# Sixteen transposes of q moved from TensorE to transposing DMAs, in a linear-attention and MLP kernel

## The chip, the cores and the metric

One core of one Trainium2 chip. The metric is the device time of one execution in microseconds (us), the median of several. PE is TensorE, PEld its weight loads, DVE is VectorE, ACT ScalarE, POOL GpSimd (which issues the loads), SP SyncE (which issues stores and transposing DMAs). All times compared below are of runs in the fast state (mean granted clock 0.99 to 1.0).

## The reference

Linear attention without a mask, a norm per head, then a layer norm and an MLP with a residual.

```python
# q, k, v: (8 batches, 8 heads, 576, 64); d_model = 512, hidden = 2048; all float32
kv  = einsum('bhsd,bhse->bhde', k, v)
o   = einsum('bhsd,bhde->bhse', q, kv)
o   = o / sqrt(mean(o*o, -1) + 1e-6) * g_norm
x   = o.transpose(0, 2, 1, 3).reshape(8, 576, 512)
xn  = (x - mean(x)) / sqrt(var(x) + 1e-6) * moe_g_ln
out = x + relu(xn @ w_ch1) @ w_ch2
```

## The kernel before

A batch has 576 rows: four slots of 128 and a fifth of 64, and the fifths of two batches share one tile. So there are 36 tiles of 128 rows: tiles 0 to 3 are batch 0, 4 to 7 batch 1, tile 8 both slots 4, tile 9 begins batch 2. Each tile needs q turned (`qT`, with the head dimension on the partitions). A slot is four blocks of 128x128. Batches 0 and 1 have q turned on PE, through PSUM; from batch 2 on, one DMA turns all five slots, 20 blocks.

```python
def add_q_turn_pe(b, t, deps, key, eng, h0=0, h1=H):
    # PE: four transposes of 128x128 into PSUM; then one copy to qT by VectorE or ScalarE
    ...
def q_turn_dma(b):                                  # batches 2 to 7
    att[b]["qT"] = work.tile([128, 20, 128], bf16, tag="qT", name="qT", bufs=3)
    nc.sync.dma_start_transpose(att[b]["qT"], qp[b % 2].rearrange("p t h d -> p (t h d)"))
...
# batch 2: q lands in qb, two copies on ScalarE reorder it into qp, then the DMA turns it
qperm.append(add("ACT", 0.85, 1.0, ok - 14, load["q", b][0:1] + [adone[b - 2]["qfree"]],
                 lambda t0=t0, t1=t1: q_permute(nc.scalar, b, t0, t1)))
...
turn = add_dma("SP", ok - 12, qperm + load["q", b] + (...), lambda: q_turn_dma(b),
               2.6e3, 1.0, occ=2.98, lat=0.25, tail=0.42)
turn.lag = 5.0 if by_slot else 0.0                  # by_slot is b >= 3: batch 2 has no lag
```

The order of instructions on every engine is fixed beforehand: a small planner in the kernel (`run_plan`) gives every step a cost and emits the steps by their planned start. Its DMAs pass through one first-in-first-out server, a transpose costing it 0.52 us per slot. The chip doesn't know the plan: each engine takes its instructions in that order and waits on semaphores.

Of the kernel before, what the change touches and what calls it, by code (L numbers as in the profile page):

```python
# [14 lines left out]
def kernel(  # L15
# [13 lines left out]
    bf16 = mybir.dt.bfloat16  # L29
# [33 lines left out]
    def no_fifth(b):  # L63
        return fifth(b + 1)
# [19 lines left out]
    work = ctx.enter_context(tc.tile_pool(name="work", bufs=2))  # L84
# [10 lines left out]
    def add(eng, occ, dur, key, deps, fn, dma=None, alloc=None, main=False, lag=0.0):  # L95
        s = Step()
        s.eng, s.occ, s.dur, s.key, s.fn = eng, occ, dur, key, fn
        s.deps = [d for d in deps if d is not None]
        s.dma, s.alloc, s.main, s.frees, s.behind = dma, alloc, main, None, None
        s.start = s.done = None  # L100
        s.lag = lag
        steps.append(s)
        return s
# [82 lines left out]
    def add_dma(eng, key, deps, fn, nbytes, rate, occ=None, lat=None, tail=None):  # L186
        if eng == "POOL":
            s = add(eng, occ or 0.67, 0, key, deps, fn, dma=(1.0, nbytes / rate / 1e3, 0.6))
        else:
            s = add(eng, occ or 0.55, 0, key, deps, fn,  # L190
                    dma=(0.6 if lat is None else lat, nbytes / rate / 1e3,
                         0.75 if tail is None else tail))
        return s
# [26 lines left out]
    qp = [consts.tile([128, 5, H, D], bf16, name=f"qp{i}") for i in range(2)]  # L220
# [56 lines left out]
    pos, okey = {}, {}  # L277
# [14 lines left out]
    att = [dict() for _ in range(B)]  # L292
    done = [dict() for _ in range(N_TILES)]
    adone = [dict() for _ in range(B)]
# [4 lines left out]
    load = {}  # L299
# [6 lines left out]
    def spread(f):  # L306
        ps = psum.tile([128, 512], f32, tag="mm", name="scale_ps", bufs=BANKS["mm"])
        nc.tensor.matmul(ps[:, 0:f.stop - f.start], lhsT=ones, rhs=scales[:, f], start=True, stop=True)
        att[0]["scale", f.start] = ps

    for eng, f, dst in (("ACT", slice(0, Dm), "gl"), ("DVE", slice(Dm, Dm + D), "gn")):
        s = add("PE", *((1.8, 2.0) if dst == "gl" else (0.4, 0.6)), -98, row + [ones_done], lambda f=f: spread(f), alloc="mm")
# [14 lines left out]
    def pool_do(occ, fn, deps=()):  # L327
        return add("POOL", occ, occ + 0.1, 0, deps, fn)
# [13 lines left out]
    def load_w_kv1():  # L342
# [26 lines left out]
    z1 = [pool_do(0.5, f) for f in (  # L369
        lambda: nc.gpsimd.memset(qp[0][no_fifth(0), 4, :, :], 0.0),  # L370
        lambda: nc.gpsimd.memset(qp[1][no_fifth(1), 4, :, :], 0.0),
        lambda: nc.gpsimd.memset(v5[0][no_fifth(0), :, :], 0.0),
        lambda: nc.gpsimd.memset(v5[1][no_fifth(1), :, :], 0.0),
        lambda: nc.gpsimd.memset(kv_pack[1], 0.0),
        lambda: nc.gpsimd.memset(kv_pack[2], 0.0),
    )]
# [32 lines left out]
    def add_q_turn_pe(b, t, deps, key, eng, h0=0, h1=H):  # L409
        w = (h1 - h0) / H  # L410
        s = add("PE", 0.24 * w, 0.24 * w + 0.26, key, [ident] + list(deps), lag=2.0 if t == 4 else 0.0, fn=
                lambda: q_turn_pe(b, t, h0, h1), alloc=("mm", "kvt")[b])
        occ, dur = act_cost(512 * w) if eng == "ACT" else dve_cost(512 * w, 1.92)
        e = add(eng, occ, dur, key, [s],
                lambda: q_turn_out(b, t, h0, h1, nc.scalar if eng == "ACT" else nc.vector))
        s.frees = e
        adone[b].setdefault(("qT", t), []).append(e)

    def q_turn_dma(b):
        att[b]["qT"] = work.tile([128, 20, 128], bf16, tag="qT", name="qT", bufs=3)  # L420
        nc.sync.dma_start_transpose(
            att[b]["qT"], qp[b % 2].rearrange("p t h d -> p (t h d)"))

    def kv_mm(b, hps):
        ps = psum.tile([128, HP, 128], f32, tag="kvt", name="kv_ps", bufs=BANKS["kvt"])
# [218 lines left out]
    for i, (h0, h1) in enumerate(((0, 4), (4, 8))):  # L644
        hps = range(h0 // 2, h1 // 2)
        s = add("PE", 0.7, 0.95, -60 + i, load["v", 0, h0] + [k0p[i]],
                lambda hps=hps, i=i: kv_mm(0, hps), alloc="kvt")
# [9 lines left out]
    load_w_kv1()  # L657
    pool_load(("q", 0, 4), load_fifth(qp[0][:, 4, :, :], q, 0), 180.0, [])
    pool_load(("q", 1, 4), load_fifth(qp[1][:, 4, :, :], q, 1), 180.0, [])
    add_q_turn_pe(0, 4, load["q", 0, 4] + [z1[0]], pos[8] - 50, "DVE")  # L660
    adone[0]["qfree"] = adone[0]["qT", 4][0]


# [1 line left out]
    def plan_batch(b):  # L665
        p = pos[FIRST[b]]
        ok = okey[FIRST[b]]
        kperm = []
        if b == 1:
            for h0, h1 in ((0, 4), (4, 8)):  # L670
                kperm.append(add("ACT", 1.2, 1.35, p - 18, load["k", 1],
                                 lambda h0=h0, h1=h1: k_permute(nc.scalar, 1, h0, h1)))
            for t in range(5):
                key = (p - 17 + 3 * t) if t < 4 else pos[8] - 40
                if t < 4:
                    qperm = add("ACT", *act_cost(512), key, load["q", 1],
                                lambda t=t: q_permute(nc.scalar, 1, t, t + 1))
                    qread = qperm
                else:
                    qperm = load["q", 1, 4][0]  # L680
                add_q_turn_pe(1, t, [qperm, z1[1]], key + 1, ("DVE", "ACT")[t % 2])
            vdeps = load["v", 1]
            adone[1]["qread"] = qread
            adone[1]["qfree"] = adone[1]["qT", 4][0]
        else:
            f = FIRST[b]
            def gate(n):

                if b >= 3:
                    m, i = divmod(n, 4)  # L690
                    pool_do(0.1, lambda: nc.gpsimd.tensor_copy(  # L691
                        mark, blk[m]["xT"][:, 0, i * 128:i * 128 + 1]), done[n]["xT"])
            def gate_turn():
                if b >= 3:
                    pool_do(0.1, lambda: nc.gpsimd.tensor_copy(
                        mark, att[b - 1]["qT"][:, 0, 0:1]), [adone[b - 1]["qfree"]])
            dk = [adone[b - 2]["kvmm"]]
            if b < 4:

                pool_do(0.5, lambda: nc.gpsimd.memset(kp[b % 2][no_fifth(b), 4, :, :], 0.0), dk)  # L700
            gate(f - 7 if b > 3 else 5)
            gate_turn()
            by_slot = b >= 3
            if by_slot:
                pool_load(("k", b), load_slots(kp[b % 2], k, b), rate1, dk)
            else:
                pool_load(("k", b), load_kv(kb, k, b), rate4, dk)
            pool_load(("k", b), load_fifth(kp[b % 2][:, 4, :, :], k, b), 180.0, dk)
            def some_q():
                gate(f - 6 if b > 3 else 6)  # L710
                if by_slot:
                    pool_load(("q", b), load_slots(qp[b % 2], q, b), rate1, [adone[b - 2]["qfree"]])
                else:
                    pool_load(("q", b), load_q(b, 0, 4), rate4, [adone[b - 1]["qread"]])
                pool_load(("q", b), load_fifth(qp[b % 2][:, 4, :, :], q, b), 180.0,
                          [adone[b - 2]["qfree"]])
            def some_v():
                gate(f - 5 if b > 3 else 7)
                pool_load(("v", b), load_kv(vb, v, b), rate4, dk)
                pool_load(("v", b), load_fifth(v5[b % 2], v, b), 100.0, dk)  # L720
            for load_some in (some_v, some_q) if b == 2 else (some_q, some_v):
                load_some()
            for h0, h1 in ((0, 4), (4, 8))[by_slot * 2:]:
                kperm.append(add("ACT", 0.85, 1.0, ok - 16, load["k", b][0:1] + dk,
                                 lambda h0=h0, h1=h1: k_permute(nc.scalar, b, h0, h1)))
            qperm = []
            for t0, t1 in ((0, 2), (2, 4))[by_slot * 2:]:
                qperm.append(add("ACT", 0.85, 1.0, ok - 14, load["q", b][0:1] + [
                    adone[b - 2]["qfree"]], lambda t0=t0, t1=t1: q_permute(nc.scalar, b, t0, t1)))
            for x in kperm + qperm:  # L730
                x.lag = 4.0 if b == 2 else 6.0
            kperm += load["k", b]
            turn = add_dma("SP", ok - 12, qperm + load["q", b] + (
                adone[b - 3].get("outs", []) if b >= 3 else []),
                           lambda: q_turn_dma(b), 2.6e3, 1.0, occ=2.98, lat=0.25, tail=0.42)
            for t in range(5):
                adone[b]["qT", t] = [turn]
            adone[b]["qfree"] = turn
            turn.lag = 5.0 if by_slot else 0.0
            adone[b]["qread"] = qperm[-1] if qperm else None  # L740
            vdeps = load["v", b]
        outs_before = adone[b - 3].get("outs", []) if b >= 3 else []
        s = add("PE", 1.12 if b > 1 else 1.34, 1.35 if b > 1 else 1.57, (p - 17.5 if b == 1 else ok - 4), vdeps + kperm,
                lambda: kv_mm(b, range(HP)), alloc="kvt")
# [214 lines left out]
```

## Time and profile before

The time was 296.15 us (three runs).

| engine | busy us | share of 295.1 us |
|---|---|---|
| PE | 283.1 | 96% |
| DVE | 165.8 | 56% |
| ACT | 143.1 | 49% |

The list of waits for PE: who waited for what, us in total, times, the longest.

```profile
PE kv_ps L429 <- DMA vb<-in_v_dram: 4.3, 1, 4.3
PE scale_ps L308 <- DMA scales<-in_moe_g_ln_dram: 2.3, 1, 2.3
PE mm_ps L598 <- DMA xT<-xc: 0.7, 1, 0.7
PE mm_ps L583 <- ACT xT L540: 0.7, 1, 0.7
PE mm_ps L583 <- DMA w<-in_moe_w_ch_dram: 0.4, 1, 0.4
```

All but the third line lie before 26 us; the third is at 175.9 us. So PE bounds the program from 26 us on. The chain of work that ended last, in order of time (start us, us, what), runs wholly on PE in the stage that the change touches:

```profile
44.42 0.22 PE qT_ps L401 x4
44.65 1.73 PE mm_ps L617 x8
...
47.46 0.22 PE qT_ps L401 x4
47.69 0.86 PE mm_ps L617 x4
48.55 0.22 PE qT_ps L401 x4
48.77 2.59 PE mm_ps L617 x12
...
52.45 0.22 PE qT_ps L401 x4
```

The four `qT_ps` lines are the 16 transposes at issue: 0.22 us for four, 0.89 us in all. A matmul of 512 columns takes 0.216 us of the chain (1.73 / 8), a transpose of 128 columns about 0.056 (0.89 / 16).

The table by stretches for the same stage has start:end, length, busy us of PE, PEld, DVE, ACT and POOL, granted clock, share of the DMA engines' time that packets took (over 1 where packets overlap), and GB/s:

```profile
45.00:50.00 5.00, 5.00 (x34) 2.64 (x33) 4.56 (x12) 1.68 (x4) 0.00 (x0) 1.00 1.59 192
...
55.00:60.00 5.00, 5.00 (x93) 5.00 (x91) 2.66 (x12) 4.67 (x11) 0.43 (x1) 1.00 0.40 116
```

The DMA engines are full of loads until about 55 us (1.59), then nearly idle (0.40). Batch 2's q is the last large load of that queue. Its line in the list of DMA issues between 40 and 43.3 us (kilobytes as written, us from issue to landing):

```profile
qb<-in_q_dram POOLq DMA_DIRECT2D x1, 512.0 KB, 11.7
```

It is issued at 42.6 us and lands at 54.3. The copies on ScalarE that need it begin at 59.5 us and wait for nothing: some 5 us of slack. Batch 2's own turn, 20 blocks (640 KB), is issued at 61.5 us, with no load beside it, and lands after 4.9 us; for some 3 us of these it moves about 215 GB/s.

### The profile page before, as it was taken

The numbers are of one execution on the slowest core, as the hardware profiler recorded it, in microseconds if no ns is written. First come the engines' busy times: TensorE is split into PE (matmuls) and PEld (weight loads), VectorE is DVE, ScalarE is ACT, GpSimd is POOL, SyncE is SP. The second block draws the span as 40 slices with busy tenths as digits, with TensorE's granted clock in tenths as the row PEclk, the third lists the DMA queues.
The fourth block names the chain that finished last, engine by engine and source line by source line (L and its number), as shares of the span: only waits on it lengthen the run. The fifth ranks groups of instructions, "written<-read, shape, count | busy, mean of one in ns | idle before, by whom it ended". The sixth has DMA issues, their size and how long they took to land.

```text
span 295.1 us, 5184 instructions
## 1 busy us (share of the span) xinstructions
PE 283.1 (96%) x2061; PEld 161.1 (55%) x2061; DVE 165.8 (56%) x360; ACT 143.1 (49%) x288; POOL 66.0 (22%) x92
## 2 busy tenths in 40 slices
PE   3799999999999999999999999999999999999995
PEld 1789955877745445444544445544454444444444
DVE  1397038759876886557655773577557755420022
ACT  3178972986857612671267117621762177006500
POOL 8882230208207024320403207020000000000000
PEclk9999999999999999999999999999999999999999
DMA  6999999749999998998399799999201310210012
GB/s 91 176 196 206 203 199 192 181 89 106 188 176 82 139 120 200 161 120 168 93 131 86 107 185 130 137 134 178 56 18 53 91 53 18 56 71 35 0 73 72
DMA packets 107388, 35.21 MB, mean 119 GB/s; under 512 B 85603, under 2 KB 103395, under 8 KB 107364
## 3 DMA queue, kind: packets, MB, share of 16 engines
q0 software_dynamic: 72608, 18.35, 65.2%
q1 hardware_dynamic: 34516, 16.39, 23.5%
q8 instruction: 16, 0.26, 0.4%
q10 hardware_dynamic: 240, 0.13, 0.2%
q14 instruction: 8, 0.07, 0.1%
HBM read 36.70 MB, written 9.44 MB: 156 GB/s over the span
## 4 chain that ended last, share of the span: by engine, by line
PE 87%; DMA 10%; POOL 1%; issue 1%; DVE 1%; ACT 0%; ACTq 0%; POOLq 0%
PE mm_ps L617 39%; PE mm_ps L598 33%; PE mm_ps L583 8%; DMA w<-in_moe_w_ch_dram 4%; DMA xT<-xc 3%; PE kv_ps L429 3%; PE out_ps L452 3%; DMA kb<-in_k_dram 3%; PE xT_ps L533 1%; PE qT_ps L401 0%; POOL qp L254 0%; POOL kb L233 0%; POOL w L334 0%; DVE ss L474 0%; POOL vb L233 0%
## 5 line engine op out<-in xcount | busy, mean ns | idle before, releaser
L617 PE MATMUL mm_ps<-w,m 128*128 128x512 bf16 (+2 forms) x608 | 130.3, 368 | 0.0
L598 PE MATMUL mm_ps<-xT,w 128*128 128x512 bf16 x448 | 100.8, 379 | 0.7 <-DMA xT<-xc 0.7
L605 ACT ACTIVATE m<-mm_ps 128x512 bf16<-128x512 f32 x112 | 66.8, 597 | 51.2 <-PE mm_ps L598 50.2
L617 PEld LDWEIGHTS <-m 128*128 128x128 bf16 x608 | 57.0, 98 | 59.7
L598 PEld LDWEIGHTS <-w 128*128 128x128 bf16 x448 | 43.0, 98 | 49.5 <-issue 1.2
L624 DVE SCALAR_TENSOR_TENSOR x<-mm_ps,rstd,x 128x512 f32<-128x512 f32 (+2 forms) x38 | 27.3, 721 | 41.9 <-PE mm_ps L617 41.8
L474 DVE TENSOR_REDUCE ss<-sq 128x8 f32<-128x512 f32 (+1 forms) x37 | 24.8, 670 | 46.0 <-ACT sq L465 45.9
L465 ACT ACTIVATE sq<-out_ps 128x512 f32<-128x512 f32 (+1 forms) x37 | 21.5, 584 | 52.3 <-PE out_ps L452 52.3
L583 PE MATMUL mm_ps<-xT,w 128*128 128x128 bf16 x512 | 30.9, 219 | 1.0 <-ACT xT L540 0.7
L583 PEld LDWEIGHTS <-w 128*128 128x128 bf16 x512 | 29.3, 98 | 2.1 <-issue 0.8
L526 DVE SCALAR_TENSOR_TENSOR xc<-x,mv,gl 128x512 bf16<-128x512 f32 (+1 forms) x37 | 27.1, 737 | 1.4 <-DVE mv L521 0.3
L469 DVE TENSOR_TENSOR xg<-out_ps,gn 128x512 f32<-128x512 f32 (+1 forms) x37 | 24.8, 669 | 0.3
L691 POOL COPY mark<-xT 128x1 bf16<-128x1 bf16 x15 | 5.1, 340 | 80.4 <-DMA xT<-xc 67.8
L590 ACT ACTIVATE m<-mm_ps 128x512 bf16<-128x512 f32 x32 | 18.3, 597 | 3.2 <-PE mm_ps L583 2.5
L504 DVE TENSOR_TENSOR x<-xg,inv 128x512 f32<-128x512 f32 x24 | 16.6, 693 | 0.8
L520 DVE BATCH_NORM_STATS2 stats<-x 128x6 f32<-128x512 f32 x24 | 16.6, 690 | 0.5
L444 DVE CAST kv_pack<-kv_ps 64x256 bf16<-64x256 f32 (+1 forms) x18 | 7.1, 392 | 15.8 <-PE kv_ps L429 15.7
L478 ACT ACTIVATE rms<-ss,eps_attn 128x8 f32<-128x8 f32 (+1 forms) x37 | 11.0, 298 | 9.9 <-DVE ss L474 9.9
L429 PE MATMUL kv_ps<-vb,kp 128*128 128x128 bf16 (+1 forms) x144 | 11.5, 231 | 4.3 <-DMA vb<-in_v_dram 4.3
L452 PEld LDWEIGHTS <-qT 128*128 128x128 bf16 x160 | 11.6, 98 | 7.3 <-DVE kv_pack L444 0.3
L452 PE MATMUL out_ps<-kv_pack,qT 128*128 128x128 bf16 x160 | 14.9, 220 | 0.1
L429 PEld LDWEIGHTS <-kp 128*128 128x128 bf16 (+1 forms) x168 | 10.9, 103 | 5.6 <-issue 2.6
(61 smaller groups left out, 171.4 us busy)
## 6 DMA issues: line engine op xcount, KB each, us to landing
out_dram<-x SPq DMA_DIRECT2D x28, 256.0 KB, 2.8
w<-in_moe_w_ch_dram POOLq DMA_DIRECT2D x8, 512.0 KB, 12.5
vb<-in_v_dram POOLq DMA_DIRECT2D x6, 512.0 KB, 9.1
kp<-in_k_dram POOLq DMA_DIRECT2D x5, 512.0 KB, 8.2
qp<-in_q_dram POOLq DMA_DIRECT2D x5, 512.0 KB, 9.5
out_dram<-x SPq DMA_DIRECT2D x14, 128.0 KB, 2.5
qb<-in_q_dram POOLq DMA_DIRECT2D x2, 512.0 KB, 15.7
qp<-in_q_dram POOLq DMA_DIRECT2D x10, 64.0 KB, 8.4
```

Source lines behind the costliest of these rows:

```text
L429: nc.tensor.matmul(ps[:, hp, :], lhsT=kp[b % 2][p, t, 2 * hp:2 * hp + 2, :].rearrange("p h d -> p (h d)"), rhs=(v5[b % 2][:, 2 * hp:2 * hp ...
L452: nc.tensor.matmul(o3[:, hp, :], lhsT=att[b]["qT"][:, 4 * t + hp, :], rhs=kv_pack[b % 3][:, hp, :], start=(i == 0), stop=(i == len(bs) - 1))
L465: nc.scalar.activation(sq[:, h0:h1, :], st[n]["ps", h0][:, h0:h1, :], func=AF.Square)
L469: nc.vector.tensor_mul(xg[:, h0:h1, :], st[n]["ps", h0][:, h0:h1, :], gn.to_broadcast([128, h1 - h0, D]))
L474: nc.vector.tensor_reduce(ss[:, h0:h1, :], st[n]["sq"][:, h0:h1, :], axis=AX.X, op=ALU.add)
L526: nc.vector.scalar_tensor_tensor(xc[:, f0:f1], in0=st[n]["x"][:, f0:f1], scalar=blk[m]["mv"][:, i, 0:1], in1=gl[:, f0:f1], op0=ALU.subtrac ...
L583: nc.tensor.matmul(ps[:, d, :], lhsT=w1[c][:, kk, d * 128:(d + 1) * 128], rhs=blk[m]["xT"][:, kk, i * 128:(i + 1) * 128], start=(kk == 0), ...
L590: nc.scalar.activation(st[n]["m1"][:, c, :, :], st[n]["m1ps", c], func=AF.Relu)
L598: nc.tensor.matmul(ps, lhsT=w1[c][:, kk, d * 128:(d + 1) * 128], rhs=blk[m]["xT"][:, kk, :], start=(kk == 0), stop=(kk == nKm - 1))
L605: nc.scalar.activation(blk[m]["m1", c][:, d, :], blk[m]["m1ps", g], func=AF.Relu)
L617: nc.tensor.matmul(st[n]["m2ps", f0], lhsT=m1_piece(n, c, d), rhs=w2[c][:, d, f0:f1], start=(c == 0 and d == 0), stop=(c == 3 and d == 3))
L624: nc.vector.scalar_tensor_tensor(x[:, f0:f1], in0=st[n]["m2ps", f0], scalar=blk[m]["rstd"][:, i, :], in1=x[:, f0:f1], op0=ALU.mult, op1=AL ...
```

## The change

The intent is to spare PE 16 transposes, and VectorE and ScalarE four copies, with DMAs on an SP queue that is empty in that stage.

```diff
-    def q_turn_dma(b):
-        att[b]["qT"] = work.tile([128, 20, 128], bf16, tag="qT", name="qT", bufs=3)
+    def q_turn_dma(b, t0=0, t1=5):
+        if "qT" not in att[b]:
+            att[b]["qT"] = work.tile([128, 20, 128], bf16, tag="qT", name="qT", bufs=3)
         nc.sync.dma_start_transpose(
-            att[b]["qT"], qp[b % 2].rearrange("p t h d -> p (t h d)"))
+            att[b]["qT"][:, 4 * t0:4 * t1, :],
+            qp[b % 2][:, t0:t1, :, :].rearrange("p t h d -> p (t h d)"))
+
+    def add_q_turn_dma(b, t0, t1, deps, key):
+        s = add_dma("SP", key, deps, lambda: q_turn_dma(b, t0, t1), 520.0 * (t1 - t0), 1.0,
+                    occ=0.6 * (t1 - t0) + 0.1, lat=0.25, tail=0.42)
+        ...
-    add_q_turn_pe(0, 4, load["q", 0, 4] + [z1[0]], pos[8] - 50, "DVE")
+    add_q_turn_dma(0, 4, 5, load["q", 0, 4] + [z1[0]], pos[8] - 41)
 ... batch 1, for t in range(5):
-                add_q_turn_pe(1, t, [qperm, z1[1]], key + 1, ("DVE", "ACT")[t % 2])
+                if t < 2:
+                    add_q_turn_pe(1, t, [qperm, z1[1]], key + 1, ("DVE", "ACT")[t % 2])
+                elif t > 2:
+                    add_q_turn_dma(1, *((2, 4) if t == 3 else (4, 5)), [qperm, z1[1]], key + 1)
```

More of the change, by code (lines that the diff above doesn't have):

```diff
@@ L417, in add_q_turn_pe @@
         adone[b].setdefault(("qT", t), []).append(e)
-    def q_turn_dma(b):
-        att[b]["qT"] = work.tile([128, 20, 128], bf16, tag="qT", name="qT", bufs=3)
+    def q_turn_dma(b, t0=0, t1=5):
+        if "qT" not in att[b]:
+            att[b]["qT"] = work.tile([128, 20, 128], bf16, tag="qT", name="qT", bufs=3)
         nc.sync.dma_start_transpose(
-            att[b]["qT"], qp[b % 2].rearrange("p t h d -> p (t h d)"))
+            att[b]["qT"][:, 4 * t0:4 * t1, :],
[3 more added lines that the diff above has]
+                    occ=0.6 * (t1 - t0) + 0.1, lat=0.25, tail=0.42)
+        for t in range(t0, t1):
+            adone[b].setdefault(("qT", t), []).append(s)
     def kv_mm(b, hps):
```

## The prediction

> **What bounds the kernel.** TensorE, at full clock. The busy-time table gives it 283.1 of 295.1 us (96%), VectorE 56%, ScalarE 49%. The list of waits gives PE four waits up to 26 us (4.3 us for v, 2.3 for the scales, 0.7 for an xT, 0.4 for a weight) and only one later, 0.7 us for an xT turned by DMA. By the table of stretches PE is 100% busy from 26 to 150 us. The Trainium skill ("Perfetto Trace Analysis", Identifying the Most-Contended Engine) warns that a busy PE may not be near its peak. Here the chain in order of time settles it: four 128x512 matmuls take 0.86 us of it, about one column per 2.4 GHz cycle, so an instruction taken off PE here should shorten the program by its own time.
>
> **Removed.** 16 of the 40 transposes on TensorE, which the timeline shows between 44.3 and 52.7 us. Each group of four is 0.22 us of the chain: 4 x 0.22 = 0.89 us, all critical. Also three evictions on VectorE (0.42 us each) and one on ScalarE (0.58 us); neither holds up PE there, so these are worth nothing.
>
> **Added.** Three transposing DMAs on SP, whose queue is empty between 2 and 51 us. A one-slot transpose (the size of an xT) takes SP 1.2 us and lands 2.4 to 6.7 us after issue, the 20-tile ones 4.9 to 10.7. By the table of stretches the DMA engines are saturated until about 55 us, so I expect the long end, 5 to 9 us. The skill ("DMA: Bandwidth & Descriptors", Issuing engines are not separate DMA queues) says that all queues share 16 engines; that spread agrees.
>
> **When.** Batch 1's slots 2 and 3 are ready when ScalarE's last copy of q ends (41.6 us), so qT lands at 48 to 50 us; tile 6 used it at 46.2. The slot-4 loads landed at about 45 us, so their turns land at 50 to 53; tile 8 uses them at 61.8. Tile 6 took 9 us from its first matmul to xT, and its main matmuls begin at 66.2: slack for some 6 us. VectorE has room from 53 to 61 us (68% busy). The plan's own DMA model puts a transpose behind all queued loads, so PE's order should place the delayed tiles late enough not to stall. Loads may slow by 1 to 2 us; batch 2's have several us of slack. GpSimd's 9.5 us wait for the old slot-4 turn should shrink to a few us and gain nothing, since PE doesn't wait for loads there.
>
> **Sum.** -0.9 us, plus 0.1 to 0.2 for a reshuffled order that adds a short wait: about 295.4 us, range 294.8 to 296.5. Faster by over 2%: 1%; within 2%: 96%; slower by over 2%: 3%.
>
> **Signs.** Right: 24 transposes of q on PE instead of 40; PE busy down by 0.9 us, to 282.2; no new PE wait of 0.3 us or more between 26 and 150 us; the new transposes land in 5 to 9 us; main matmuls from about 60 us on start 0.9 us earlier and stay so to the end. Wrong: PE waiting for qT between 42 and 70 us, or for an xT of tile 6, 7 or 8.
>
> **What would make it wrong.** PE takes instructions in order, so a transpose that lands later than planned stalls it directly; one held behind the deep queue of loads (they took 11 to 20 us to land) could cost 2 to 5 us. A new order could move or add an xT wait. SP issues in order: a turn waiting for its load can hold back another turn.

## The result, and the profile after

The time is 295.78 us (six runs, 295.06 to 296.00) against 296.16: a ratio of 0.9989, 95% interval 0.9967 to 1.0011. A ratio is the mean time of one kernel's fast runs over that of the other's of the same rounds, so not quite the ratio of the medians. The change was run twice more, in later sets of rounds: 0.9999 (0.9966 to 1.0031) and 0.9988 (0.9964 to 1.0012). The mean of the three ratios, 0.9992, is 0.24 us: less than a third of the 0.89 us taken off PE, and not clear of zero in any of the rounds.

The list of waits for PE after (the line numbers are 8 to 11 higher):

```profile
PE kv_ps L437 <- DMA vb<-in_v_dram: 2.9, 1, 2.9
PE scale_ps L308 <- DMA scales<-in_moe_g_ln_dram: 2.3, 1, 2.3
PE mm_ps L591 <- ACT xT L548: 0.7, 1, 0.7
PE out_ps L460 <- DMA qT<-qp: 0.5, 1, 0.5
```

A new wait stands in the last line. The chain of work that ended last, in order of time:

```profile
41.45 19.31 DMA qb<-in_q_dram
60.77 0.02 issue
60.79 0.03 ACT qp L381
60.81 0.93 issue
61.74 1.04 ACT qp L381
62.78 0.03 ACT sq L473
62.81 6.49 DMA qT<-qp
69.30 0.04 issue
69.34 0.62 PE out_ps L460 x8
```

The chain no longer runs on PE here. It runs through batch 2's load of q (19.31 us in place of 11.7), the two copies on ScalarE that now have to wait for it, batch 2's turn, and only then PE. PE's timeline shows the hole; the bracket is its idle time and what ended it:

```profile
67.86 1.03 PE L625 MATMUL mm_ps<-w,m 128*128 128x512 bf16 x4
69.34 0.62 PE L460 MATMUL out_ps<-kv_pack,qT 128*128 128x128 bf16 x8 [0.45 <-DMA qT<-qp]
```

The four matmuls give way to the next after 0.86 us, so at 68.72: 0.62 us are lost (the bracket's 0.45 counts only from the modelled end of the last matmul, 0.17 us later: 1.03 - 0.86). The stretches and the issues of before, after the change:

```profile
45.00:50.00 5.00, 5.00 (x28) 2.38 (x26) 4.40 (x10) 0.71 (x2) 0.00 (x0) 1.00 1.61 146
...
55.00:60.00 5.00, 5.00 (x82) 4.53 (x80) 3.26 (x10) 4.22 (x10) 0.00 (x0) 1.00 1.25 242
```

```profile
qb<-in_q_dram POOLq DMA_DIRECT2D x1, 512.0 KB, 19.3
qT<-qp SPq DMA_TRANSPOSE x1, 10.1
```

While the transposes are in flight the DMA engines are as full as before (1.61 against 1.59) but move 146 GB/s in place of 192, and they catch up only between 55 and 60 us, where they used to be nearly idle.

**A ruler for the traces.** The span of the profiled run fell by 1.8 us (295.1 to 293.3), but 1.1 us of that is the start: the first long run of first-layer matmuls (80 in a row), which waits for weights in either kernel, began at 24.8 us and not at 25.9. In all traces that point lies anywhere from 24.6 to 25.9 us, whatever the kernel. So traces are compared from there: to the first product of batch 2's k and v ("to kv"; the 16 transposes come before it); to the first second-layer run after block 2's first layer, at about 100 us ("early stage"); and from there to the last matmul ("rest"). All are differences of times in PE's timeline: of starts, and for "rest" up to the end of the last matmul.

| kernel | to kv | early stage | rest | batch 2's q, issue to landing | PE's waits after 26 us |
|---|---|---|---|---|---|
| before, two traces | 36.35, 36.52 | 75.40, 75.56 | 190.28, 190.04 | 11.7, 12.1 | 0.69, 0.46 at 175 us |
| the change, three traces | 35.46 in each | 75.24, 75.46, 75.70 | 189.50, 189.42, 189.42 | 19.3, 19.4, 19.6 | 0.45, 0.53, 0.60 for batch 2's qT; in the third also 0.26 for an xT from ScalarE |

PE's work did shrink as predicted: "to kv" is 0.89 us shorter in the first trace, to the hundredth. By the end of the early stage this is gone. A second difference, in the rest, comes back below.

The sharpest measure lies between the first two columns, from kv to the end of the early stage, since the 16 transposes come before it: 39.05 and 39.04 us before, but 39.78, 40.00 and 40.24 with the change. By the start times two holes in PE's timeline make up the difference. One is for batch 2's qT: 0.62, 0.69 and 0.77 us in the three traces. The other, at 64 to 65 us, is for the xT of tile 6: 0.11, 0.25 and 0.42 us. ScalarE copied that xT late, because it had stood 1.05, 1.20 and 1.36 us at its copies of batch 2's q. So the late load reaches PE by two ways, and the later it landed (19.3, 19.4, 19.6 us), the larger both holes. The list of waits shows the second in one trace only.

### The profile page after: what moved, and what is told of

The parts are those of the page before. It is cut to its first block, busy times and chain, and to the rows that moved or that the text cites. A ratio compares the mean times of both kernels' runs of the same rounds, so it can differ in the third digit from the quotient of the medians.

```text
span 293.3 us, 5159 instructions
## 1 busy us (share of the span) xinstructions
PE 282.9 (96%) x2045; PEld 160.8 (55%) x2045; DVE 165.0 (56%) x357; ACT 142.8 (49%) x287; POOL 65.4 (22%) x92
## 4 chain that ended last, share of the span: by engine, by line
PE 75%; DMA 16%; POOL 5%; ACT 1%; issue 1%; DVE 0%; POOLq 0%
PE mm_ps L625 36%; PE mm_ps L606 33%; DMA qb<-in_q_dram 13%; PE out_ps L460 2%; DMA qT<-qp 2%; PE kv_ps L437 2%; PE mm_ps L591 1%; POOL qp L254 1%; ACT qp L381 1%; POOL w L334 1%; POOL kb L233 1%; POOL vb L233 1%; POOL w L336 0%; PE xT_ps L541 0%; POOL v L372 0%
## 5 line engine op out<-in xcount | busy, mean ns | idle before, releaser
L598 ACT ACTIVATE m<-mm_ps 128x512 bf16<-128x512 f32 x32 | 18.5, 598 | 2.4 <-PE mm_ps L591 1.7
L437 PE MATMUL kv_ps<-vb,kp 128*128 128x128 bf16 (+1 forms) x144 | 11.8, 234 | 2.9 <-DMA vb<-in_v_dram 2.9
## 6 DMA issues: line engine op xcount, KB each, us to landing
qb<-in_q_dram POOLq DMA_DIRECT2D x2, 512.0 KB, 19.6
```

Source lines behind the costliest of these rows:

```text
L437: nc.tensor.matmul(ps[:, hp, :], lhsT=kp[b % 2][p, t, 2 * hp:2 * hp + 2, :].rearrange("p h d -> p (h d)"), rhs=(v5[b % 2][:, 2 * hp:2 * hp ...
L598: nc.scalar.activation(st[n]["m1"][:, c, :, :], st[n]["m1ps", c], func=AF.Relu)
```

## The experiments

Theory A: the new transposes hold up the loads that share the DMA engines, batch 2's q and its turn come late, and PE gives the gain back. Theory B: the new order of instructions costs it. Theory C: nothing is given back, and only noise hides the gain.

### The kernel before and the change, again

No edit. Expected:

> The kernel before, unchanged, for its noise and a second trace. I divide a trace in three: the start, up to the run of 80 first-layer matmuls of 128 columns (25.9 us in the first trace); the early stage, up to the first second-layer run of 20 matmuls (101.5 us); the rest, up to the last matmul (291.6 us). First trace: 25.9, 75.6, 190.1 us. All theories: ratio to itself 0.998 to 1.002, early stage 75.6 +- 0.1 us, the start 24.8 to 26.0 us. Open: whether the 0.7 us wait for an xT at 175 us is there again; if it is, it belongs to the kernel, if not, it is chance.

> The change, unchanged, a second trace and a tighter time. First trace: start 24.8, early stage 75.4, rest 189.35 us; PE waits 0.45 us for batch 2's qT at 69.3 us. Theory A (the new transposes delay the loads queued beside them, so that batch 2's q and its turn come late, and PE gives back 0.6 to 0.7 of the 0.89 us): the wait is there again, 0.3 to 0.9 us, the load of batch 2's q takes 18 to 20 us to land again, the early stage is 75.3 to 75.6 us, the time 0.2 to 0.5 us under the kernel before. Theory C (the full 0.9 us is gained and only noise of the start hides it): no such wait, early stage 74.7 us, time 0.8 to 1.0 us lower.

Measured: 295.89 us (ratio to the same kernel 1.0015, 0.9973 to 1.0057) and 295.93 us (0.9999, 0.9966 to 1.0031). So a ratio of one kernel to itself was 0.15% off, which is half of what is being looked for: the traces have to carry the argument. The early stage repeats to 0.16 us in the kernel before, and to 0.46 us over the three traces of the change (the table above). The change's wait for qT is there again (0.53 us), and batch 2's q again needs 19.4 us. Theory C falls: the early stage is not 74.7 us. The prior trace's wait at 175 us is there again in the kernel before, 0.46 us.

### Extra transposes in the kernel before

All 40 transposes stay on PE; the three DMAs of the change are added, into a buffer that is overwritten before use. I compared the order of instructions with that of the kernel before: the same on PE, DVE, ACT and POOL.

```diff
+    def extra_turn(b, t0, t1):
+        ...
+        nc.sync.dma_start_transpose(
+            att[2]["qT"][:, c:c + 4 * (t1 - t0), :],      # batch 2's qT: overwritten later
+            qp[b % 2][:, t0:t1, :, :].rearrange("p t h d -> p (t h d)"))
+    def add_extra_turn(b, t0, t1, deps, key):
+        add("SP", 0.7, 0.7, key, deps, lambda: extra_turn(b, t0, t1))   # costs the plan nothing
```

> The kernel before, with all 40 transposes on PE and the same instructions in the same order on PE, VectorE, ScalarE and GpSimd, plus the three transposing DMAs of the change, issued where the change issues them, but writing into batch 2's qT, which is overwritten before use. The result is right. Theory A: batch 2's q lands 18 to 20 us after its issue in place of 11.7, its turn lands at about 70 us, PE, which wants it at 68.0 us, waits 1.5 to 3 us, and the kernel is 1.5 to 3 us slower than before. Theory B (not the DMA traffic but the plan's new order gives the gain back) and theory C: within 0.3 us of the kernel before, no new wait on PE.

Measured: a median of 298.12 us over six runs, five fast ones from 296.46 to 299.82 us and a slow one of 302.57 us, which the ratio leaves out: 1.0072 (1.0029 to 1.0115). The profiled run was the fastest of them, and even its early stage is 76.46 us, 1.0 us longer than the mean of before. From the DMA issues between 40 and 43.3 us, and from the list of waits for PE:

```profile
qb<-in_q_dram POOLq DMA_DIRECT2D x1, 512.0 KB, 19.3
```

```profile
PE mm_ps L584 <- ACT xT L541: 1.1, 2, 0.7
```

Theory A's cause is shown by itself: with the order untouched, three transposing DMAs delay the load from 11.7 to 19.3 us and cost time. My expectation of the form was partly wrong: PE's wait in this trace was mostly not for qT. ScalarE, which also works in order, stood 2.4 us at its copy of batch 2's q, and PE then waited 0.46 us (at 65.6 us) for an xT that ScalarE had yet to evict. By the start times PE lost 0.62 us there and 0.31 us at its first matmuls with batch 2's qT, against an expected 1.5 to 3 us. From kv to the end of the early stage the trace takes 39.99 us, in place of 39.05. (The other 0.7 us of the line lie in the start, as in the kernel before.)

### No turn at all

The change without its DMAs; the tiles concerned read the qT of slots 0 or 1, so the result is wrong (relative error 0.39).

```diff
-        s = add_dma("SP", key, deps, lambda: q_turn_dma(b, t0, t1), 520.0 * (t1 - t0), 1.0, ...)
         for t in range(t0, t1):
-            adone[b].setdefault(("qT", t), []).append(s)
+            adone[b].setdefault(("qT", t), []).append(deps[0])
```

> The change without its three transposing DMAs: the four slots are not turned at all, and their tiles read the qT of slots 0 or 1 instead, so the result is wrong on purpose. PE does the work of the changed kernel. Theory A: nothing is given back: batch 2's q lands about 12 us after its issue, no wait of PE for qT, early stage 74.6 to 74.8 us, time 0.8 to 1.0 us under the kernel before and 0.4 to 0.7 under the change. Theory B: the wait or a like one stays and the time is that of the change. Theory C: as the change, 0.9 us under the kernel before.

Measured: batch 2's q lands after 11.8 us, no wait for qT, and the early stage is 74.51 us: 0.97 us under the mean of before (75.48), as theory A expected. The time, 295.09 us, ratio 0.9968 (0.9933 to 1.0004), was the lowest of that chip's four kernels. But the profiled run was the slowest of the six (296.91 us; it has a wait of 1.8 us at 175.8 us: that wait again). From kv to the end of the early stage it takes 39.05 us: nothing is lost. These two runs speak against theory B: the DMAs cost time without a new order, and PE's smaller work costs none without the DMAs. One gap remains: the plan was made anew without the DMAs, so the order on PE, VectorE and ScalarE is not quite that of the change (the built programs differ in places), and the change's own order was never run without them. But in the change's traces the two holes, both at something that came late with batch 2's q, account for the whole loss.

### The same bytes as plain copies

As the extra transposes, with `dma_start` in place of `dma_start_transpose`, same source and destination tiles.

> The kernel before plus the three extra DMAs, as in the run with extra transposes, but as plain copies of the same bytes between the same tiles. If the bytes or the number of DMAs cause the delay: batch 2's q again lands 18 to 20 us after issue and the early stage is again about 76.5 us, the time 1 to 3 us up. If it is the transposing that is slow (my guess: 0.5 MB of transposes cost some 6 us of the queue, which at the 200 GB/s of that stage should be 2.6 us): batch 2's q lands 12.5 to 15 us after issue, early stage 75.4 to 75.8, time within 0.5 us of the kernel before.

Measured: 295.78 us, ratio 1.0006 (0.9992 to 1.002), early stage 75.75 us. From the DMA issues between 40 and 43.3 us:

```profile
qb<-in_q_dram POOLq DMA_DIRECT2D x1, 512.0 KB, 14.3
qT<-qp SPq DMA_DIRECT2D x1, 256.0 KB, 7.2
```

Copies delay the load by 2.4 us, transposes of the same bytes by 7.5 us (19.4 against 11.9, the means). The copies cost PE nothing from kv to the end of the early stage (39.05 us). So it is the transposing that delays the load, not the bytes or the number of DMAs. Two limits belong to this. Transposes are not slow by themselves: batch 2's own turn, with no load beside it, moved about 215 GB/s, more than the 192 of the stage with loads. And they come in other packets: between 40 and 61 us the run with extra transposes has 2138 more packets under 512 bytes than the kernel before, the run with copies 44 more. Whether the transposing or the small packets slow the mix, no run here separates. As an estimate from these runs: 7.5 us / 16 is about 0.47 us of delay per block on average, against the 0.056 us that PE spends on it.

### The readers of batch 2's qT moved later

One constant of the plan, tried with 3 and with 2 us. The DMAs are those of the change.

```diff
-            turn.lag = 5.0 if by_slot else 0.0
+            turn.lag = 5.0 if by_slot else 2.0
```

> The change, with batch 2's turn planned 3 us later (one constant of the plan: the lag of that turn). PE's order then has the first matmuls that read batch 2's qT after two more second-layer groups and two groups of transposes (about 1.3 us of PE work); the DMAs are those of the change. Theory A (DMA contention makes batch 2's q and qT late, and PE gives the gain back in the one wait of 0.5 us at 69 us): qT lands as late as in the change, but PE no longer waits for it; the early stage falls from 75.3 to 74.5 to 74.8 us, against 75.5 of the kernel before; the time is 0.5 to 0.9 us under the kernel before, if the other wait, at 175 us, is like that of the kernel before. Theory B (the new order itself costs): early stage 75.2 us or more. If the early stage is 74.6 and the time is still that of the kernel before, the rest is lost after 100 us.

> As the run with 3 us, with 2 us: the first readers of batch 2's qT come after one more second-layer group (0.86 us of PE work). Theory A: no wait or one under 0.2 us at about 69 us, early stage 74.5 to 74.9 us; time as with 3 us. Also a further look at the wait at 175 us, which three kernels showed with 0.2 to 1.8 us and the two traces of the change did not: if it is chance, one of these runs will show it.

Measured with 2 us: 295.05 us, ratio 0.9974 (0.9959 to 0.999). With 3 us: 295.22 us, ratio 0.9991 (0.9974 to 1.0007). The load is as late as in the change (19.5 and 18.5 us), but PE no longer waits for qT, and the early stages are 75.13 and 74.97 us. That is longer than expected (74.5 to 74.9). Up to kv, PE's weight loads stood 0.23 and 0.46 us for ScalarE's copies at about 40 to 42 us, before the readers that the lag moves. From kv on, the version with 2 us takes 39.44 us and that with 3 us 39.05: the first still lost 0.40 us for the xT of tile 6, since the lag moves the readers of qT and not ScalarE's copies. The version with 2 us was run again on one chip with the change:

> The change once more, on one chip with the two versions that beat the kernel before, and a third trace. Open so far: its two traces show 0.8 us less than the kernel before from the 80 matmuls to the end (no wait at 175 us), its times (295.8 and 295.9 us against 296.2 and 295.6) no gain. If the traces were lucky runs: here a wait at 175 us of 0.2 to 1.8 us, and a time within 0.3 us of the kernel before. If the gain is real: time 0.5 us or more lower. Theory A in both cases: wait for batch 2's qT at about 69 us, 0.3 us or more; the two other versions are 0.3 to 0.8 us faster than this one in the same rounds.

> The change with batch 2's turn planned 2 us later, again, same chip and rounds as the change: the same DMAs, only a later place for the readers of batch 2's qT. Theory A: no wait for qT, 0.3 to 0.8 us faster than the change, ratio to the kernel before 0.996 to 0.9985.

Measured: the change 295.42 us, ratio 0.9988 (0.9964 to 1.0012), with a wait of 0.60 us for qT; the version with 2 us 294.76 us, ratio 0.997 (0.9944 to 0.9996), early stage 74.84 us. The means of those six runs each are 295.45 and 294.92 us, a ratio of 0.9982. From the six values each, a 95% interval of that difference is about 0.53 +- 0.55 us (my estimate), so this comparison by itself is not quite clear of zero. From kv to the end of the early stage the trace takes 39.09 us. PE's timeline of the second run with 2 us, where the wait used to be:

```profile
68.30 1.89 PE L625 MATMUL mm_ps<-w,m 128*128 128x512 bf16 x8
70.03 0.61 PE L460 MATMUL out_ps<-kv_pack,qT 128*128 128x128 bf16 x8
```

Eight matmuls come first, not four, and the readers of qT begin without a bracket. This is the best kernel that gives the right result: 0.3% under the kernel before in both of its rounds, each interval clear of 1. The early stage accounts for 0.35 and 0.64 us of the 0.8 to 0.9 us; its traces also lack the wait at 175 us, for which no cause is known (below).

### Half of the change

Only batch 1's slots 2 and 3 by DMA, or only the two slots 4: 8 blocks each.

```diff
-                if t < 2:
+                if t < 2 or t == 4:     # first half;  the second half: if t < 4, and DMA for t == 4
```

> A part of the change: only batch 1's slots 2 and 3 (8 of the 16 transposes) turned by DMA, the two slots 4 left on PE. PE's work is 0.44 us under the kernel before. Theory A, with a delay in proportion to the blocks transposed: batch 2's q lands 15 to 16 us after issue, its turn 3 us earlier than in the change, no wait or a short one, early stage 75.0 to 75.3. If the delay comes from any transpose in that stage and not from their number: 18 us or more, and a wait as in the change. Theory C: early stage 75.1.

> Only batch 1's slots 2 and 3 by DMA, again, same chip and rounds: 0.44 us less PE work than the kernel before, no wait for qT. Theory A: 0.4 to 0.8 us under the kernel before, so faster than the whole change although it takes half as much off PE.

> The other half: only the two slots 4 by DMA (8 transposes in two DMAs, issued at about 45 us), slots 2 and 3 of batch 1 on PE. Theory A with a delay by the number of blocks: batch 2's q lands 14 to 17 us after issue (11.7 without, 19.4 with all 16, 17.3 with slots 2 and 3), its turn starts by 62 us, no wait for qT or a short one, time 0.2 to 0.6 us under the kernel before. If the slot-4 turns are the ones that hurt (batch 2's last load waits for them): 18 us or more and a wait of 0.3 us or more, time that of the kernel before.

Slots 2 and 3: 294.89 us, ratio 0.9973 (0.996 to 0.9985), and 295.10 us, ratio 0.9996 (0.9962 to 1.003; two of six runs were at 296.6 and 296.9). Batch 2's q landed after 17.3 and 16.3 us, and PE waited for no qT in either trace (early stage 75.21 and 74.95 us): half the transposes, and the slack is nearly, but not quite, used up. In the rounds that it shared with the whole change the means were 295.57 and 295.45 us, so the expected advantage over the whole was not seen.

Slots 4: 295.51 us, ratio 1.0003 (0.9968 to 1.0037). The load landed after 14.3 us, and PE didn't wait for qT. So both halves stay within the slack, and the whole doesn't: the slots 4 are not the ones that hurt. Nor is the delay the same for every block: 8 blocks of slots 2 and 3 delayed the load by 5.4 and 4.4 us (15 to 16 us to landing had been expected for them), 8 of the slots 4 by 2.4 us. The 0.47 us per block is an average, not a rate. From kv to the end of the early stage the three traces of the halves take 39.04 or 39.05 us. The trace of the slots 4 shows no gain in the early stage (75.56 us), since PE's weight loads stood 0.7 us at about 40 us for ScalarE's copies of batch 1's q, before the DMAs at issue began. It also has the longest of the waits at 175 us, 2.2 us.

### What stays open

The wait at 175 us, for an xT of block 5, was 0.69 and 0.46 us in the kernel before, 0.23 with the extra transposes, 1.8 without turns and 2.2 with the slots 4 alone. It was absent in three traces of the change, three with a lag, two with slots 2 and 3, and one with plain copies. It follows neither from the early stage nor from the number of transposes. Nor does it follow from the order of instructions at that place: in the built programs of all nine kernels here, the order on every engine is the same from about 112 us on. Kernels traced more than once showed it each time or never, so that it is pure chance isn't shown either. A profile is one run, and a wait of 0 to 2 us can explain much of the spread of the times, but the unprofiled runs have no trace to show it. It also makes the change's traces 0.5 to 0.9 us shorter from the ruler's start to the last matmul (264.7 to 265.1 against 265.6 and 265.7 us), while its times were only 0.24 us lower. Whether the unprofiled runs of the kernel before mostly lack that wait, or those of the change mostly have one, no run here shows.

## Why the prediction was right or wrong

- **The time: inside the range.** 295.4 us (294.8 to 296.5) was predicted, 295.78 measured. The forecast of "within 2%" held. But the range also holds the time before, 296.16 us, so to fall inside it says little about the mechanism, and in part it was luck. The gain was predicted as 0.75 us; the three ratios give 0.24 us on average, not clear of zero.
- **What bounds the kernel, and the 0.89 us: right.** "To kv" fell from 36.35 to 35.46 us, and the run without turns kept it (early stage down by 0.97 us). The transposes of q on PE are 24 in place of 40, as predicted. PE's busy time fell only from 283.1 to 282.9 us, not to 282.2; why is open.
- **Landing of the new transposes: a little short.** 5 to 9 us were predicted; the first took 10.1, the other two a median of 8.6. Tile 6, 7 and 8 had the slack claimed for them: PE waited for none of their qT. The xT of tile 6 did come 0.11 to 0.42 us late, but because ScalarE stood at batch 2's q.
- **The failed step: "Loads may slow by 1 to 2 us; batch 2's have several us of slack."** Batch 2's q, the load that mattered, slowed by 7.5 us, and the slack was about 5. I took the transposes to be so many bytes; the plain copies (2.4 us) show that this would have been nearly right for bytes. Nor did batch 2's own turn in the trace before give a warning, since it ran alone at about 215 GB/s: the cost lies in transposes and loads side by side. The new wait followed, 0.45 to 0.60 us, where the prediction said that none of 0.3 us or more would come. In its signs of being wrong, "PE waiting for qT between 42 and 70 us" came true, but for batch 2's qT, not for the slots that had moved; so did, by the smaller hole, "for an xT of tile 6".
- **The plan's order: right for the moved tiles, wrong for the next.** The transposes were placed behind the queued loads in the plan, as predicted, and the moved tiles did not stall PE. But the plan charges its server 0.52 us per slot, 2.1 us for the four, and the load behind them lost 7.5. So the plan put batch 2's readers too early, and a lag of 2 us mended the wait for qT. Raising the charge itself was not tried.
- **The allowance of 0.1 to 0.2 us for a short wait** is the term of the sum that was mis-sized: the early stage gave back nearly all of the 0.89 us (75.47 us on average over the change's three traces, against 75.48 before).
- **GpSimd's wait for the slot-4 turn: wrong, and harmless.** It was to shrink from 9.5 us to a few, and it grew to 11.0. The load that it held back (batch 2's slot 4) landed at 61.0 us, still 1.8 us before ScalarE's copies were done. The Trainium skill ("DMA: Bandwidth & Descriptors", Queues, rings and completion order) says that an engine takes the queues in turn, packet by packet. The trace agrees as far as it goes: the first transpose, issued within 1 us of batch 2's q, landed after 10.1 us, the load after 19.3. That taking turns with the transposes is how the load was delayed would fit this, but no run here shows the turns themselves.

## What to carry to other kernels

Before moving work from a busy engine to DMAs, ask which transfer is last in the queue in that stage, how much slack its reader has, and what the new DMAs cost that queue, measured beside its loads and not by bytes: here a block cost PE 0.056 us and the load behind it about 0.47 us on average. Look for the new wait at the next consumer of the shared queue, not at the data that was moved, and remember that an engine in order (ScalarE here) can carry a late load to PE by another way. When a static order meets a later landing, moving the readers may keep the gain where the DMAs themselves can't be made faster.

## What the Trainium skill lacked or had wrong

- "DMA: Bandwidth & Descriptors" has nothing on what a transposing DMA between SBUF tiles does to loads beside it. It says that for such traffic the fabric side (435 GB/s) binds, and its table of measured facts (Latency and other measured facts) gives 261 GB/s for a DMA transpose in one kernel and 350 to 400 GB/s for contiguous ones, without saying between which memories. At 261 GB/s, 512 KB would take 2.0 us (an estimate from that page). Here 16 blocks (512 KB) of transposes delayed a queued load by 7.5 us, the same bytes as plain copies by 2.4 us, and the engines' traffic fell from 192 to 146 GB/s at the same busy share. With no load beside it, a turn of 640 KB moved about 215 GB/s.
- The same page (Rules for kernel authors) says that a transpose next to ordinary DMAs needs nothing. For correctness this agrees with these runs (every run with transposes that was meant to be right was right); for time it does not: 1.0072 as the ratio with three extra transposes.
- "TensorE: Matmul & The Clock Gate" (Back-to-back issue gap) gives a sustained 81 ns for matmuls of 128 columns and 131 ns for 512, and calls its formula, 56 and 216 ns, one for isolated matmuls. In this kernel's continuous stream the spacing was 55.6 ns (16 first-layer matmuls in 0.89 us of the chain) and 216 ns: the formula held, the sustained figures did not. Another section of the page (Wait — 56ns, not 53.3ns?) has it so for back-to-back matmuls, 55.6 and 215.7 ns: the page disagrees with itself.
